# Decode step, one core: w_down's last rows on all partitions, wo's last row product sent straight to the output rows, and no closing barrier

## The chip, the cores and the metric

One core of one Trainium2 chip. The metric is the device time of one execution in microseconds (us); a kernel's figure is the median of its runs. With one core there is no second die to compare. Every change that this document talks about is below 0.4% of the time, so two instruments are used side by side: medians of runs taken in the same rounds, and distances between events in the trace of one execution.

Some words that are used throughout. A semaphore is a counter on which an engine waits. A transfer has landed when the last of its parts (sixteen for each weight) has been counted on its semaphore. A matmul keeps one operand (the weights) in the tensor engine and streams the columns of the other, the moving operand, past it; its results go to PSUM. The granted clock is the share of the tensor engine's full clock that the profile records.

## The reference

```python
x  = A_x                                   # 1 x 1 x 640
xn = layernorm(x)
q  = (xn @ wq)                             # 32 heads of 128
p  = softmax(q @ k_cache^T * 128**-0.5)    # 32 heads, 32768 keys each
o  = p @ v_cache
h  = silu(xn @ w_gate) * (xn @ w_up)       # 1728 hidden units
out = x + o @ wo + h @ w_down              # 1 x 1 x 640, bf16
```

The caches of keys and values are 8 MB per head each, 537 MB together, and are read once. All the rest is small: wq 5.2 MB, w_gate and w_up 2.2 MB each, w_down 2.2 MB, wo 5.2 MB.

## The kernel before

The kernel streams the caches through a ring of three 64 KB slots per partition. After the last head comes a tail: the feed-forward weights (gate, up, down), then wo in six pieces, are read into the same ring, and the products end in one 128x5 accumulator `acc` (5 columns of 128 outputs). These are the parts that the change touches.

```python
    WTAIL = [8, 8, 8, 5, 2, 1]            # wo: rows per partition in each piece, 32 in all
    ...
    # DMA queue, tail. 1728 = 13 * 128 + 64, so FM = 13, FL = 64, FB = 14
    e.dma_start(wg, ...).then_inc(s_ffn[0], 16)
    e.dma_start(wu, ...).then_inc(s_ffn[1], 16)
    e.dma_start(flat[:, d0:d0 + FM * D], B_w_down[0:FM * 128, :].rearrange(
        "(p j) n -> p (j n)", j=FM)).then_inc(s_ffn[2], 16)
    e.dma_start(wd[0:FL, FM, :], B_w_down[FM * 128:F, :]).then_inc(s_ffn[2], 16)   # 64 partitions
    ...                                                         # then wo, piece by piece
    e.wait_ge(s_fin, 2)
    e.dma_start(out[...], orow[:, :]).then_inc(s_out, 16)

    # tensor engine, tail
    hidden_part(0); ...; hidden_part(1); down(); project().then_inc(s_att, 1)
    def project():
        for i, n in enumerate(WTAIL):
            t.wait_ge(s_wo[i], 16)
            for _ in range(n):
                for c in range(NCD):       # NCD = 5; the moving operand has one column
                    mm = t.matmul(acc[:, c:c + 1], lhsT=wo_v[:, j, c, :], rhs=ot[:, j:j + 1], ...)
                j += 1
    t.wait_ge(s_fin, 1)
    t.matmul(orow_ps, lhsT=outb[:, :], rhs=ident[:, :], start=True, stop=True).then_inc(s_or, 1)  # turn

    # vector engine, tail
    v.wait_ge(s_att, 1)
    v.tensor_tensor(out=outb[:, :], in0=xr[:, :], in1=acc, op=ALU.add).then_inc(s_fin, 1)
    v.wait_ge(s_or, 1)
    v.tensor_copy(out=orow[:, :], in_=orow_ps).then_inc(s_fin, 1)

    # GpSimd, end
    g.wait_ge(s_out, 16)                   # the output has landed; then a barrier of all engines
```

## Time and profile before

| | before |
|---|---|
| median of 3 runs | 1288.11 us (1288.03 to 1288.64) |
| span in the profile | 1286.3 us |
| read from HBM | 553.99 MB, 431 GB/s over the span |
| busy share: tensor, vector, scalar engine | 81%, 52%, 4% |

The first lines are from the page of the kernel before. Each row of the first two cuts the span into 40 slices: the granted clock of the tensor engine in tenths, then GB/s. The third is the chain of waits, by engine.

```profile
PEclk9799888898888999888898888898888998888895
...
GB/s 424 424 450 427 429 438 431 430 430 444 428 432 442 428 432 434 436 428 432 442 430 432 436 432 430 430 444 428 432 442 428 432 432 438 428 432 442 430 417 355
...
DMA 53%; PE 30%; DVE 11%; issue 6%; DVEq 0%; SPq 0%
```

The DMA rate is level from the first slice to the 38th (424 to 450 GB/s). Only the last two slices sag (417, 355), and in the last one the granted clock falls to 0.5. The page's row of DMA shares, in tenths, reads 9 in every slice but the last, which is 8. So the place to look for a gain without reading less is the end, the last 64 us.

The table of stretches of the kernel before, for the tail (start:end and length in us, then busy time and instruction count of each engine, granted clock, DMA share, GB/s):

```profile
core 0: us, PE busy (x) PEld busy (x) DVE busy (x) ACT busy (x) POOL busy (x), PEclk, DMA share, GB/s
1260.00:1265.00 5.00, 4.79 (x128) 4.70 (x128) 0.51 (x2) 0.00 (x0) 0.00 (x0) 0.50 1.01 426
1265.00:1270.00 5.00, 3.62 (x59) 3.60 (x60) 0.00 (x0) 0.20 (x1) 0.00 (x0) 0.50 1.00 380
1270.00:1275.00 5.00, 3.52 (x73) 3.45 (x72) 0.93 (x8) 0.23 (x2) 0.00 (x0) 0.50 0.98 398
1275.00:1280.00 5.00, 3.63 (x130) 3.52 (x127) 0.00 (x0) 0.00 (x0) 0.00 (x0) 0.50 1.00 415
```

The DMA engines are busy throughout (share 0.98 to 1.01), but between 1265 and 1275 they move less: 380 and 398 GB/s. That is where w_down arrives. A share near 1 says that engines have packets under way, not that they move bytes at their best rate.

The end of the chain of waits of the kernel before, in order of time (start, length in us, what):

```profile
1253.07 29.08 DMA ring<-in_A_wo_dram
1282.15 0.05 issue
1282.19 1.49 PE ps L414 x40
1283.68 0.03 issue
1283.71 0.05 DVEq L602
1283.76 0.04 issue
1283.81 0.17 DVE outb L603
1283.98 0.04 issue
1284.02 0.28 PE ps L439
1284.30 0.02 issue
1284.33 0.28 DVE orow L605
```

L414 are the 40 matmuls of wo's last three pieces, L603 the sum with x, L439 the turn from 128x5 to 5x128, L605 the copy out of PSUM. The view merges the last three pieces into one DMA wait; by the semaphore records of the trace they landed at 1282.15, 1282.93 and 1283.33. The same records put the output's landing at 1285.82, GpSimd's sight of it at 1285.85 and the end of the closing barrier at 1286.26. The last semaphore record of the execution, which belongs to the runtime and not to the kernel, is at 1288.18; the measured time of this execution was 1288.06.

### The profile page before, as it was taken

How to read it: one execution, taken by the hardware profiler on the slowest of the kernel's cores; microseconds unless marked ns; L12 is line 12 of the kernel's file. 1: busy time of each engine (PE TensorE's matmuls, PEld its weight loads, DVE VectorE, ACT ScalarE, POOL GpSimd, SP SyncE). 2: the span in 40 equal slices, each digit the busy share in tenths (PEclk: the TensorE clock that was granted, in tenths of full speed). 3: DMA queues.
4: the chain of work that ended last, by engine and by line, in shares of the span. 5: the costliest groups of instructions: out<-in, count | busy, mean ns of one | idle time of the engine just before them, and what ended most of it. 6: DMA issues, size and time to landing. Idle time of an engine off the chain costs nothing.

```text
span 1286.3 us, 9864 instructions
## 1 busy us (share of the span) xinstructions
PE 1041.6 (81%) x5153; PEld 261.4 (20%) x3234; DVE 670.4 (52%) x409; ACT 52.2 (4%) x140; POOL 2.5 (0%) x17
## 2 busy tenths in 40 slices
PE   4599777789777788777798777788777798778797
PEld 1011112221112221112221112221112221112227
DVE  0855665445665445664446664446664446654440
ACT  2000000000000000000000000000000000000000
POOL 0000000000000000000000000000000000000000
PEclk9799888898888999888898888898888998888895
DMA  9999999999999999999999999999999999999998
GB/s 424 424 450 427 429 438 431 430 430 444 428 432 442 428 432 434 436 428 432 442 430 432 436 432 430 430 444 428 432 442 428 432 432 438 428 432 442 430 417 355
DMA packets 11192, 554.17 MB, mean 431 GB/s; under 512 B 1259, under 2 KB 1452, under 8 KB 1708
## 3 DMA queue, kind: packets, MB, share of 16 engines
q1 hardware_dynamic: 11178, 554.00, 99.7%
q8 instruction: 9, 0.15, 0.0%
q14 instruction: 3, 0.02, 0.0%
q10 hardware_dynamic: 2, 0.00, 0.0%
HBM read 553.99 MB, written 0.00 MB: 431 GB/s over the span
## 4 chain that ended last, share of the span: by engine, by line
DMA 53%; PE 30%; DVE 11%; issue 6%; DVEq 0%; SPq 0%
DMA ring<-in_A_k_cache_dram 51%; PE ps L327 17%; PE ps L295 11%; DVE ring L543 10%; DMA ring<-in_A_wo_dram 2%; PE ps L314 1%; PE ps L369 0%; PE ps L363 0%; PE ps L357 0%; PE ps L414 0%; SPq L239 0%; DVEq L543 0%; DVE sc L549 0%; DVE pmax L555 0%; DVEq L188 0%
## 5 line engine op out<-in xcount | busy, mean ns | idle before, releaser
L543 DVE TENSOR_TENSOR ring<-ring,qb 128x8192 bf16<-128x8192 bf16 x128 | 557.8, 4420 | 316.4 <-DMA ring<-in_A_k_cache_dram 316.4
L295 PE MATMUL ps<-ring,ident 128*128 128x512 bf16 x1920 | 496.4, 417 | 0.0
L327 PE MATMUL ps<-ring,P 128*4 128x512 bf16 x1984 | 443.3, 379 | 0.0
L314 PE MATMUL ps<-ring,ident 128*128 128x512 bf16 x128 | 55.9, 437 | 220.7 <-DVE ring L543 220.2
L327 PEld LDWEIGHTS ps<-ring,P 128*4 128x4 bf16 x1984 | 163.4, 85 | 237.8
L314 PEld LDWEIGHTS ps<-ring,ident 128*128 128x128 bf16 x128 | 12.6, 98 | 618.0 <-DVE ring L543 345.0
L549 DVE TENSOR_REDUCE sc<-ps 128x64 f32<-128x512 f32 x128 | 82.3, 684 | 62.6 <-PE ps L295 62.6
L561 DVE TENSOR_SCALAR negb<-ps 128x1 f32<-128x1 f32 x32 | 5.1, 158 | 108.4 <-PE ps L369 108.4
L466 ACT ACTIVATE P<-sc,negb 128x256 bf16<-128x256 f32 x32 | 16.2, 507 | 956.7 <-DVE negb L561 956.7
L558 DVE TENSOR_REDUCE m<-ps 1x1 f32<-1x128 f32 x32 | 8.9, 278 | 85.2 <-PE ps L363 85.2
L349 PEld LDWEIGHTS ps<-identf,o 4*128 4x128 f32 x248 | 30.6, 190 | 13.1 <-issue 13.1
L349 PE MATMUL ps<-identf,o 4*128 4x1 f32 x248 | 33.2, 251 | 0.0
L357 PEld LDWEIGHTS ps<-rsum,ones 128*128 128x128 f32 x64 | 12.1, 190 | 99.0 <-issue 98.2
L457 ACT ACTIVATE o<-ps,rzb 4x512 f32<-4x512 f32 x31 | 21.0, 678 | 6.2 <-PE ps L327 6.2
L287 PE MATMUL ps<-ring 128*128 128x512 bf16 x39 | 11.3, 458 | 10.9 <-DMA ring<-in_A_wq_dram 10.9
L462 ACT ACTIVATE ocol<-ps 128x1 f32 (+1 forms) x31 | 5.4, 173 | 222.2 <-PE ps L349 222.2
L555 DVE TENSOR_REDUCE pmax<-sc 128x1 f32<-128x256 f32 x32 | 13.4, 420 | 0.0
L363 PE MATMUL ps<-identf,pmax 128*1 128x128 f32 x64 | 12.2, 273 | 1.2 <-DVE pmax L555 1.2
L369 PE MATMUL ps<-m,ones 1*128 1x1 f32 x64 | 12.1, 256 | 0.4 <-DVE m L558 0.4
L369 PEld LDWEIGHTS ps<-m,ones 1*128 1x128 f32 x64 | 9.4, 182 | 14.2 <-issue 13.5
L393 PE MATMUL ps<-xn,ring 128*128 128x1 bf16 (+1 forms) x140 | 8.9, 198 | 1.6 <-issue 1.6
L531 DVE RECIPROCAL rzb<-ps 128x1 f32<-128x1 f32 x32 | 5.1, 159 | 8.1 <-PE ps L357 8.1
(62 smaller groups left out, 80.8 us busy)
## 6 DMA issues: line engine op xcount, KB each, us to landing
ring<-in_A_wq_dram SPq DMA_DIRECT2D x1, 5120.0 KB, 15.3
ring<-in_A_v_cache_dram SPq DMA_DIRECT2D x1, 4096.0 KB, 31.8
ring<-in_A_wo_dram SPq DMA_DIRECT2D x3, 1280.0 KB, 25.0
ring<-in_B_w_gate_dram SPq DMA_DIRECT2D x1, 2160.0 KB, 22.9
ring<-in_B_w_up_dram SPq DMA_DIRECT2D x1, 2160.0 KB, 27.7
ring<-in_B_w_down_dram SPq DMA_DIRECT2D x1, 2080.0 KB, 31.7
ring<-in_A_v_cache_dram SPq DMA_DIRECT2D x1, 2048.0 KB, 36.4
ring<-in_A_v_cache_dram SPq DMA_DIRECT2D x2, 1024.0 KB, 39.4
```

Source lines behind the costliest of these rows:

```text
L295: return t.add_instruction(mybir.InstMatmult(start_tensor_calc=False, stop_tensor_calc=stop, tile_size=(128, 128), tile_position=(0, 0), l ...
L314: t.matmul(ob, lhsT=ident[:, :], rhs=src, start=True, stop=False)
L327: mm = t.matmul(O, lhsT=P[:, h % PR, j:j + W], rhs=ring[:, s, j * DH:(j + W) * DH], start=(j == 0), stop=(j + W == NJ))
L349: mm = t.matmul(fold_ps, lhsT=o4[:, m * DH:(m + 1) * DH], rhs=identf[0:W, m:m + 1], start=(m == 0), stop=(m == W - 1))
L357: t.matmul(misc[:, 129:130], lhsT=ones[:, :], rhs=rsum[:, h % SR:h % SR + 1], start=True, stop=True).then_inc(s_z, 1)
L363: t.matmul(misc[0:1, 0:128], lhsT=pmax[:, h % SR:h % SR + 1], rhs=identf[:, :], start=True, stop=True).then_inc(s_t, 1)
L369: t.matmul(misc[:, 128:129], lhsT=ones[0:1, :], rhs=m1[0:1, h % SR:h % SR + 1], start=True, stop=True).then_inc(s_b, 1)
L457: a.activation(out=o4[:, :], in_=O, func=ACTF.Copy, scale=rzb[0:W, h % SR:h % SR + 1]).then_inc(s_o4, 1)
L466: a.activation(out=P[:, h % PR, :], in_=sc[:, :], func=ACTF.Exp, bias=negb[:, h % SR:h % SR + 1], scale=c_scale, accum_out=rsum[:, h % SR: ...
L543: v.tensor_tensor(out=kh, in0=kh, in1=q[:, None, :].to_broadcast([128, HF, DH]), op=ALU.mult).then_inc(s_mul, 1)
L549: v.tensor_reduce(out=sc[:, i * HF:(i + 1) * HF], in_=bank[i].rearrange("p (j e) -> p j e", e=G), axis=AX.X, op=ALU.add).then_inc(s_red, 1)
L555: v.tensor_reduce(out=pmax[:, h % SR:h % SR + 1], in_=sc[:, :], axis=AX.X, op=ALU.max).then_inc(s_max, 1)
```

## The change

Three things, in one diff:

1. **w_down's last 64 rows.** Each row of 640 is split into two halves, so that 64 rows become 128 half rows on all 128 partitions. The hidden units that multiply them must then stand twice, once per half; the vector engine makes doubled copies of the last 64 columns of w_gate and w_up so that the matmul delivers them that way. A mask of zeros and ones (`par`) then keeps each half row to its own half of the outputs.
2. **wo's last row.** The product of the last piece (one row per partition) no longer goes into the columns of `acc`. Five matmuls with 128 moving columns write it straight into the 5x128 output rows, and the turned sum of all the rest is added there. The intent is that the sum on the vector engine no longer stands behind the last landing.
3. **No closing barrier.** The instructions of the program's last block are emptied.

```diff
-        e.dma_start(wd[0:FL, FM, :], B_w_down[FM * 128:F, :]).then_inc(s_ffn[2], 16)
+        e.dma_start(wdr, B_w_down[FM * 128:F, :].rearrange(
+            "f (t n) -> (f t) n", t=2)).then_inc(s_ffn[2], 16)
 ...
+    def twice(i):                                   # vector engine
+        v.wait_ge(s_ffn[i], 16)
+        v.tensor_copy(out=wt[i].rearrange("p c (f t) -> p c f t", t=2),
+                      in_=(wg_v, wu_v)[i][:, :, FM * 128:F][:, :, :, None].to_broadcast(
+                          [128, NCD, FL, 2])).then_inc(s_twice, 1)
 ...  (the vector stages of silu, one instruction each instead of two, but for the last; down() in halves)
-    for i, n in enumerate(WTAIL):
+    for i, n in enumerate(WTAIL[:-1]):
 ...
+    def rows():
+        t.wait_ge(s_dg, 1)
+        t.wait_ge(s_wo[-1], 16)
+        for c in range(NCD):                        # dg: the last column of ot, one 128x5 block per c
+            t.matmul(orow_ps, lhsT=dg[:, c * NCD:(c + 1) * NCD], rhs=wo_v[:, OC - 1, c, :],
+                     start=(c == 0), stop=False, skip_group_check=True)
+        t.wait_ge(s_fin, 1)
+        return t.matmul(orow_ps, lhsT=accs[:, :], rhs=identf[:, :], start=False, stop=True,
+                        skip_group_check=True)      # accs is fp32
 ...
-    t.wait_ge(s_fin, 1)
-    t.matmul(orow_ps, lhsT=outb[:, :], rhs=ident[:, :], start=True, stop=True).then_inc(s_or, 1)
+    rows().then_inc(s_or, 1)
 ...
+    nc.main_func.blocks[-1].instructions = []
```

## The prediction

> **What bounds the kernel.** DMA. The page gives a DMA share of 9 in every slice and 431 GB/s over a span of 1286.3 us; 553.99 MB are read, and the change reads the same bytes. So only the last 25 us can change. There the chain of waits ends: wo's DMA (to 1282.15), 1.49 us of matmuls for its last 8 rows, the sum with x on the vector engine, one matmul that turns it, a copy, the output DMA. From the trace: wo's last three pieces land at 1282.15, 1282.93 and 1283.33; the 5 matmuls of the last piece end at 1283.68, the sum at 1283.98, the turn at 1284.30, the copy at 1284.62; the output DMA lands at 1285.82; the closing barrier ends at 1286.26. The other 1.9 us are the runtime's.
>
> **1. w_down's last 64 rows (the largest term).** The table of stretches shows 426 GB/s in 1260-1265, 380 in 1265-1270, 398 in 1270-1275, 424 in 1275-1278. The dip is where the 64-partition transfer of w_down runs: in the packet records the 10240-byte packets then take 490-517 ns instead of 389, those of 16640 bytes up to 807 instead of 622. The Trainium skill, "SBUF — State Buffer", section on the DMA port swizzle, says partitions 0 to 63 reach only 8 of 16 ports. The dip agrees. At the rates before and after it (gate to up 5.15 us for 2160 KB, wo pieces 3.09 us for 1280 KB) wo's first piece should have landed on its slowest engine at about 1273.4, but landed at 1274.01. Estimate: 0.57 us earlier for every later landing, net of twice as many packets of half the size (0.03). It lies wholly on the critical path, since wo's landings are waited for.
>
> **2. Direct last row.** Removed: 5 matmuls of about 27 ns and the vector engine's sum behind the last landing. Added behind it: 5 matmuls with 128 moving columns, and an fp32 turn of two passes in place of one bf16 pass. The granted clock is 0.50 there. The bf16 turn (128 columns) took 0.27 us, one with 1 column 0.165, so 0.105 us per 128 columns. An fp32 pass started 0.110 us after the other at clock 1.00; estimate 0.21 each at 0.50. After the last landing: 0.04 + 5x0.107 + 2x0.21 + 0.18 = 1.18 us, against 0.97 before (1283.33 to 1284.30). So this part loses 0.2 us.
>
> **3. No closing barrier.** GpSimd sees the output at 1285.85; the barrier ends at 1286.26. The runtime keeps its own (the Trainium skill, "Runtime: NRT & Kernel Launch", preamble/postamble breakdown). Gain 0.3 us, as the branch stays; between 0.15 and 0.6.
>
> **Off the path.** FFN matmuls and their vector stages: one instruction per stage saves about 0.2 us, but the tensor engine waits 1.6 us for wo afterwards. The duplicating copies (0.8 us each, as the 640-element copy at the start) fit idle time.
>
> **Sum:** -0.57 + 0.2 - 0.3 = about -0.7 us: 1287.4 us, range 1286.8 to 1288.1. Faster by over 2%: 0.005; same: 0.99; slower: 0.005.
>
> **Would show it right:** about 420 GB/s through 1265-1275; wo's last landing near 1282.8; the turn's end about 1.2 us after it; no barrier after GpSimd's last wait. **Wrong:** dip still there (not ports); landing-to-turn under 0.97 us (the row really is a gain); an instruction-fetch stall ("issue" idle, 0.5 to 1.6 us in this tail) moving behind the last landing; end-to-end gain from the barrier nil.

## The result, and the profile after

| | before | after |
|---|---|---|
| median of 4 runs each, same rounds | 1288.07 us (1287.97 to 1288.64) | 1287.62 us (1287.51 to 1287.67) |
| span in the profile | 1286.3 us | 1285.7 us |

The ratio is 0.9995, with a 95% interval of 0.9978 to 1.0013: by that the two are the same. All four runs after lie below all four before; a later repeat in other rounds gave 1287.68 against 1288.06. The gain is about 0.4 us, a thirtieth of one per cent.

The page of the kernel after, the same three lines:

```profile
PEclk9799888898888898888998888898888998888995
...
GB/s 424 425 451 427 427 436 437 430 428 444 428 430 438 434 432 426 444 428 430 438 434 432 426 444 428 430 442 430 432 428 442 428 430 444 430 430 428 444 412 362
...
DMA 53%; PE 29%; DVE 11%; issue 6%; DVEq 0%; SPq 0%
```

Nothing moved in the body of the kernel, as intended. The stretches of the tail:

```profile
core 0: us, PE busy (x) PEld busy (x) DVE busy (x) ACT busy (x) POOL busy (x), PEclk, DMA share, GB/s
1260.00:1265.00 5.00, 4.56 (x123) 4.47 (x120) 1.34 (x3) 0.00 (x0) 0.00 (x0) 0.50 1.02 433
1265.00:1270.00 5.00, 4.11 (x72) 4.12 (x73) 1.01 (x2) 0.20 (x1) 0.00 (x0) 0.50 0.97 405
1270.00:1275.00 5.00, 3.54 (x100) 3.48 (x99) 1.04 (x6) 0.18 (x1) 0.00 (x0) 0.50 1.01 422
1275.00:1280.00 5.00, 3.02 (x101) 2.83 (x98) 0.00 (x0) 0.00 (x0) 0.00 (x0) 0.50 1.00 414
```

From 380 and 398 the rate rose to 405 and 422. The extra 25 and 24 GB/s over 5 us each are 0.25 MB, which at 430 GB/s is 0.57 us.

The end of the chain of waits:

```profile
1253.28 28.38 DMA ring<-in_A_wo_dram
1281.65 0.05 issue
1281.70 1.23 PE ps L431 x35
1282.92 0.04 issue
1282.96 0.69 PE ps L440 x5
1283.65 0.44 PE ps L443 x2
1284.09 0.02 issue
1284.12 0.28 DVE orow L635
```

The wo DMA now ends 0.50 us earlier (1281.65 for 1282.15). The sum on the vector engine has left the chain, as was intended. But L440 (the five wide matmuls, 0.69 us) and L443 (the fp32 turn, two instructions, 0.44 us more) have come in. The timeline of the kernel after shows the same three side by side (start, length, engine, line, operation, count, and in brackets the idle time before it with what ended it):

```profile
1282.96 0.69 PE L440 MATMUL ps<-ring,dg 128*5 128x128 bf16 x5
1283.03 0.16 DVE L633 TENSOR_TENSOR accs<-xr,ps 128x5 f32<-128x5 f32 x1 [9.84 <-PE ps L431]
...
1283.45 0.63 PE L443 MATMUL ps<-identf,accs 128*5 128x128 f32 x2
```

The sum is done at 1283.19, while the tensor engine still streams the wide matmuls until 1283.65. Hiding the sum worked, but what took its place is longer: from the last landing to the end of the turn it is 1.27 us, for 0.97 before (next table).

To compare many kernels, the tail is cut at five events read from the semaphore records of each trace: w_up's last landing, wo's last landing, the end of the turn, GpSimd's sight of the output, and the last record of the execution (us):

| kernel | up to wo's last landing | last landing to turn | turn to GpSimd's sight | sight to last record |
|---|---|---|---|---|
| before | 18.19 | 0.97 | 1.54 | 2.33 |
| after | 17.58 | 1.27 | 1.54 | 2.16 |
| difference | -0.61 | +0.30 | 0 | -0.17 |

The three parts of the change fall into three different columns. They sum to -0.48; w_up itself landed 0.10 later in the profiled execution after, so the last record came 0.39 us earlier (1287.79 for 1288.18).

### The profile page after: what moved, and what is told of

It reads as the page before. It is cut to its first block, busy times and chain, and to the rows that moved or that the text cites. A ratio compares the mean times of both kernels' runs of the same rounds, so it can differ in the third digit from the quotient of the medians.

```text
span 1285.7 us, 9856 instructions
## 1 busy us (share of the span) xinstructions
PE 1045.5 (81%) x5155; PEld 261.5 (20%) x3236; DVE 672.3 (52%) x410; ACT 52.1 (4%) x139; POOL 2.6 (0%) x18
## 4 chain that ended last, share of the span: by engine, by line
DMA 53%; PE 29%; DVE 11%; issue 6%; DVEq 0%; SPq 0%
DMA ring<-in_A_k_cache_dram 51%; PE ps L340 17%; DVE ring L566 11%; PE ps L308 10%; DMA ring<-in_A_wo_dram 2%; PE ps L327 1%; PE ps L382 0%; PE ps L376 0%; PE ps L370 0%; PE ps L431 0%; SPq L251 0%; DVEq L566 0%; DVE sc L572 0%; PE ps L440 0%; PE ps L443 0%
## 5 line engine op out<-in xcount | busy, mean ns | idle before, releaser
L406 PE MATMUL ps<-xn,ring 128*128 128x1 bf16 x140 | 8.4, 196 | 1.3 <-issue 1.3
```

## The experiments

All twelve kernels gave correct results. Theory A is the prediction's: w_down gains through the SBUF ports, the row form loses at the half clock, the barrier gains a little. Rivals: B, the barrier alone gives the measured gain; C, the row form is a gain; D, the barrier gives nothing; E and F, the DMA dip is not about partitions but about bytes or packet sizes; G, the order of the waits and not the clock sets the row form's cost.

### Each part alone, and the change without its row part

Edits: the first has only hunk 1 of the diff above, the second only hunk 2, the third only hunk 3. The fourth has hunks 1 and 3:

```diff
 (against after)
-    for i, n in enumerate(WTAIL[:-1]):
+    for i, n in enumerate(WTAIL):
 ...
-    rows().then_inc(s_or, 1)
+    t.wait_ge(s_fin, 1)
+    t.matmul(orow_ps, lhsT=outb[:, :], rhs=ident[:, :], start=True, stop=True).then_inc(s_or, 1)
```

What was expected of w_down alone:

> Only w_down's last rows on all partitions (with the copies and hidden units on 128 rows that it needs); the last row of wo stays in columns and the closing barrier stays. Theory A (ports): 0.57 us faster than before, about 1287.5; the dip to 380 and 398 GB/s in 1265-1275 is gone, wo's last landing lies near 1282.8, and landing to turn stays 0.97 us. Rival B (the barrier alone gives the 0.45 us that was measured): within 0.1 us of before.

Of the row alone:

> Only wo's last row straight to output rows. Theory A: the five wide matmuls and the fp32 turn run at half clock, so last landing to end of turn grows from 0.97 to about 1.26 us and the kernel is 0.3 us slower than before, about 1288.4. Rival C (the row form is a gain, as its authors meant, since the sum leaves the tail): last landing to turn below 0.97 us and the time below before's.

Of the barrier alone:

> Only the closing barrier removed. Theory A: from GpSimd's sight of the output to the end 2.33 us in before, 2.16 us in after, so 0.17 us faster than before, about 1287.9, the rest of the trace unchanged. Rival B: 0.45 us faster. Rival D (the runtime's own barrier takes as long): no change, within 0.05 us.

Of the change without the row part:

> After without the row part: w_down on all partitions and no closing barrier, the last row in columns as before. Theory A: 0.29 us faster than after, about 1287.3, so faster than both kernels; landing to turn back to 0.97 us. Rival C: slower than after.

Measured, five runs each beside nine of before on the same chip (before: 1288.14 us, 1287.83 to 1288.23):

| kernel | median (range), us | to before | up to last landing | landing to turn | sight to last record |
|---|---|---|---|---|---|
| w_down alone | 1287.46 (1287.28 to 1287.57) | -0.68 | 17.61 | 0.95 | 2.33 |
| row alone | 1288.31 (1288.19 to 1288.45) | +0.17 | 18.32 | 1.27 | 2.33 |
| no barrier alone | 1287.83 (1287.65 to 1287.96) | -0.31 | 18.21 | 0.97 | 2.16 |
| w_down and no barrier | 1287.24 (1287.16 to 1287.57) | -0.90 | 17.60 | 0.94 | 2.25 |

Each part moves its own column of the trace, and the other columns stay within 0.13 us of before. The 2.25 in the last row is such a deviation: over all fourteen traces this column reads 2.33 with the closing barrier (once 2.42) and 2.16 without it (twice 2.24 to 2.25). w_down is the gain (rival B falls: the barrier alone gives less than half of what w_down gives, and w_down gains with the barrier in place). The row form costs 0.30 us in the trace; in the time it costs 0.17 us here, which the runs of this round alone would hardly separate from noise, so it was tested once more below. Rival C falls by the trace. The barrier is worth 0.17 us in the trace and 0.2 to 0.3 us in the medians; D falls.

The medians do not add up as the columns do. Alone, the parts make -0.68, +0.17 and -0.31, in sum -0.82, while the whole change measured -0.45. In the fourteen traces w_up's landing, before which no part of the change acts on the DMA queue, lies anywhere from 1264.90 to 1265.35; that spread enters every time, but no column. So the sizes of the parts are taken from the columns, and a difference of medians below some 0.3 us is not read as a size.

### Why w_down gained: partitions, bytes or packet size

First, the disputed transfer is issued five times instead of once, in each of its two forms (the copies land in unused columns):

```diff
 (against before)
         e.dma_start(wd[0:FL, FM, :], B_w_down[FM * 128:F, :]).then_inc(s_ffn[2], 16)
+        for i in range(4):
+            u = d0 + (FB + i) * D
+            e.dma_start(flat[0:FL, u:u + D], B_w_down[FM * 128:F, :]).then_inc(s_ffn[2], 16)
 (against after)
+        for i in range(4):
+            u = u0 + 2 * NCD * 128 + i * (D // 2)
+            e.dma_start(flat[:, u:u + D // 2], B_w_down[FM * 128:F, :].rearrange(
+                "f (t n) -> (f t) n", t=2)).then_inc(s_ffn[2], 16)
```

> Before, with the transfer of w_down's last 64 rows to partitions 0 to 63 issued five times in place of once (four more into unused columns of the same partitions, 0.33 MB more). Theory A (ports): each such transfer costs 0.6 to 0.8 us of landing time, of which 0.19 is its bytes, so 2.4 to 3.2 us slower than before, about 1291. Rival E (the dip has nothing to do with this transfer, only the bytes count): 0.8 to 0.9 us slower, 1289.

> After, with its transfer of w_down's last rows to all 128 partitions issued five times in place of once (the same 0.33 MB more, in packets of 640 bytes). Theory A: each costs its bytes and its packets' overhead alone, 8 packets of 32 ns on each engine, 0.26 us, so 1.0 us slower than after, about 1288.7. A dip like before's, or 2.4 us, would say that small transfers as such are slow and the partitions are not the cause.

Second, the 64 partitions of before are kept but the packets made as short as those of after:

```diff
 (against before)
+        wdg = flat[0:FL, w0:w0 + 2 * 384].rearrange("p (t n) -> p t n", t=2)[:, :, 0:D // 2]
 ...
-        e.dma_start(wd[0:FL, FM, :], B_w_down[FM * 128:F, :]).then_inc(s_ffn[2], 16)
+        e.dma_start(wdg, B_w_down[FM * 128:F, :].rearrange(
+            "f (t n) -> f t n", t=2)).then_inc(s_ffn[2], 16)
 ...  (the matmuls read the two halves)
```

> Before, with the 64 rows still on partitions 0 to 63 but each in two packets of 640 bytes (the halves lie 128 bytes apart in the row). It has after's packet size and before's partitions. Theory A (ports): the dip stays, 10240-byte packets near 500 ns in 1268-1270, up's landing to wo's last landing stays at 18.2 us, the time within 0.15 us of before. Rival F (the packet size or the packet count cured it): dip gone, 17.6 us, 0.6 us faster.

Measured beside nine runs of before (1288.03 us, 1287.96 to 1288.57):

| kernel | median (range), us | up to wo's first piece landed | up to wo's last |
|---|---|---|---|
| before (trace above) | | 8.87 | 18.19 |
| 64 partitions, five times | 1292.32 (1292.07 to 1293.32) | 12.05 | 22.23 |
| after (trace above) | | 8.30 | 17.58 |
| 128 partitions, five times | 1288.51 (1288.33 to 1288.53) | 9.18 | 18.58 |
| 64 partitions, packets of 640 bytes | 1288.13 (1288.06 to 1288.23) | 8.90 | 18.23 |

Up to wo's first piece, four more transfers to 64 partitions cost 3.18 us, 0.80 each; four more to 128 partitions cost 0.88 us, 0.22 each. The bytes alone, 82 KB at 430 GB/s, are 0.19. The one transfer of the change should then gain 0.80 - 0.22 = 0.58, and it gained 8.87 - 8.30 = 0.57. The five-fold kernel was 4.29 us slower than before, where 0.8 to 0.9 us were expected of rival E, which falls, and 2.4 to 3.2 us of theory A, which was too low as well (see below). Rival F falls too: short packets on 64 partitions leave time and landings where they were.

The stretches, of 64 partitions five times, then of 128 five times, then of 64 with short packets:

```profile
1265.00:1270.00 5.00, 3.57 (x58) 3.54 (x59) 0.00 (x0) 0.20 (x1) 0.00 (x0) 0.50 1.00 330
1270.00:1275.00 5.00, 3.40 (x67) 3.30 (x67) 0.93 (x8) 0.23 (x2) 0.00 (x0) 0.50 1.03 245
1275.00:1280.00 5.00, 2.95 (x97) 2.71 (x93) 0.00 (x0) 0.00 (x0) 0.00 (x0) 0.50 1.01 423
```

```profile
1265.00:1270.00 5.00, 4.23 (x74) 4.24 (x75) 0.94 (x2) 0.20 (x1) 0.00 (x0) 0.50 0.99 395
1270.00:1275.00 5.00, 3.54 (x100) 3.47 (x99) 1.03 (x6) 0.18 (x1) 0.00 (x0) 0.50 1.03 427
```

```profile
1265.00:1270.00 5.00, 4.19 (x68) 4.16 (x69) 0.00 (x0) 0.20 (x1) 0.00 (x0) 0.50 1.02 379
1270.00:1275.00 5.00, 3.51 (x83) 3.44 (x82) 0.93 (x8) 0.23 (x2) 0.00 (x0) 0.50 0.96 394
```

With five transfers the dip deepens to 245 GB/s at an unchanged DMA share of 1.03, and ends with the transfers (423 in the next stretch). Short packets on 64 partitions give the dip of before almost to the digit (379, 394 for 380, 398). The packet records show that the large packets of the neighbouring transfers are slow while the small ones run. Mean time of one packet in ns, worked out from those records (4 to 33 packets for each figure of a kernel), for packets that start from 1268 to 1269 us (w_down's main part, 16640 bytes) and from 1269 to 1270 us (wo's first piece, 10240 bytes):

| kernel | 16640 bytes | 10240 bytes |
|---|---|---|
| undisturbed | 622 | 389 |
| before (64 partitions) | 807 | 517 |
| 64 partitions, short packets | 786 | 537 |
| 64 partitions, five times | 1198 | 841 |
| after (128 partitions) | 621 | 388 |
| 128 partitions, five times | 620 | 385 |

The five-fold kernel lost 4.3 us, more than the 3.2 us of its landings up to wo's first piece. The rest is at the very end: its last wo piece landed 1.26 us after the one before it (0.40 in before). Thirteen of its sixteen parts had landed by 1286.32 and fifteen by 1286.64, the last only at 1287.49. An instruction fetch of 16384 bytes ran on the DMA engines from 1285.21 to 1286.31. That it sat in front of that one part is a guess; the records do not name the engine.

### Why the row form lost: columns at half the clock

The turn is made in bf16 instead of fp32, one pass for two:

```diff
 (against after)
-        accs = sbt("accs", [128, NCD], F32)
+        accs = sbt("accs", [128, NCD], BF16)
 ...
-        return t.matmul(orow_ps, lhsT=accs[:, :], rhs=identf[:, :], start=False, stop=True, ...)
+        return t.matmul(orow_ps, lhsT=accs[:, :], rhs=ident[:, :], start=False, stop=True, ...)
```

> After, with the turned sum in bf16: one pass of 128 columns in place of two fp32 passes. Theory A (the row form pays for columns at half clock): a pass of 0.107 in place of two of 0.213 us, landing to turn falls from 1.26 to about 0.95 us, 0.3 us faster than after, about 1287.3, level with the kernel that has no row part. If the vector engine's sum or something else were what ends last there, nothing changes.

Measured: 1287.39 us (1287.23 to 1287.57), in the rounds of the three kernels above, 0.64 below before. Landing to turn fell from 1.27 to 0.95 us as expected. So the tensor engine's columns were what ended last. The row form then costs as much as the column form (0.95 against 0.94 to 0.97), which is no gain either. So at an unchanged clock of 0.50 what the fp32 turn takes beyond a bf16 turn (0.32 us) accounts for the whole loss; the half clock sets what each column costs, but is not by itself what made this form lose.

The other half of the theory is the clock. In two kernels, the tensor engine is given work while it waits, so that the full clock may be granted at the end:

```diff
 (against after, and against the bf16 turn)
+    def busy(n):
+        for _ in range(n):
+            t.matmul(bank[1], lhsT=ident[:, :], rhs=qb[:, 0:512], start=True, stop=True)
 ...
     def down():
         t.wait_ge(s_ffn[2], 32)
+        busy(3)
 ...
         for i, n in enumerate(WTAIL[:-1]):
+            busy({2: 7}.get(i, 0))
             t.wait_ge(s_wo[i], 16)
```

> After, with matmuls of 512 columns into an unused bank where the tensor engine waits anyway: 3 before the hidden units are ready, 7 before wo's third piece. They are meant to have the clock granted at 1.00 at the end. Theory A (the row form loses because its columns run at half clock): where the profile shows 1.00 behind the last landing, the wide matmuls start 0.056 apart instead of 0.107 and the turn's passes 0.110 instead of 0.213, landing to turn falls from 1.26 to about 0.75 us, 0.5 us faster than after, 1287.1. If the clock stays at 0.50: nothing changes, since all ten fit into waits (1.4 and 1.85 us, then 0.7). Rival G (the order of the waits, not the clock, sets landing to turn): 1.26 us even at clock 1.00.

> The same ten matmuls in the kernel with the bf16 turn. Theory A: at clock 1.00 landing to turn is about 0.56 us (0.04, six matmuls at 0.056, 0.18) against 0.95 without them, 0.4 us faster than that kernel, about 1287.0, and faster than the kernel without the row part, since only then is the row form the cheaper one. At clock 0.50: level with the bf16 turn alone.

Measured beside before at 1288.19 us (1287.93 to 1288.39): 1289.47 us with the fp32 turn and 1288.76 us with the bf16 turn, both slower than before. The expectation that the ten matmuls fit into waits was wrong. The tensor engine's timeline of the first shows why:

```profile
1275.35 2.31 PE L437 MATMUL ps<-ot,ring 128*128 128x1 bf16 x79
1279.39 0.18 PE L437 MATMUL ps<-ot,ring 128*128 128x1 bf16 x1 [1.74 <-issue]
1279.43 3.15 PE L412 MATMUL ps<-qb,ident 128*128 128x512 bf16 x7
```

The wait before wo's third piece was not free. 1.74 us of it is "issue", an engine that waits for nothing the profile shows; it ends after an instruction fetch of 16384 bytes (1277.03 to 1278.09 in the DMA records). The fillers stood behind that stall and began at 1279.43, and by the time they were through, at 1282.4, the third and fourth piece had long landed (1279.48, 1281.46).

As a measurement of the clock the pair still worked, because only the second was granted it in its profiled execution. Why the first was not, with the same ten matmuls, no run shows. Its stretches (columns as above):

```profile
1282.00:1284.00 2.00, 2.00 (x61) 1.68 (x59) 0.00 (x0) 0.00 (x0) 0.00 (x0) 0.72 0.05 12
1284.00:1286.00 2.00, 1.11 (x29) 0.81 (x25) 0.44 (x2) 0.00 (x0) 0.00 (x0) 1.00 0.00 0
```

The end of the timeline, first of the bf16 turn alone (clock 0.50), then of the bf16 turn with fillers (clock 1.00):

```profile
1282.84 0.69 PE L440 MATMUL ps<-ring,dg 128*5 128x128 bf16 x5
...
1283.33 0.31 PE L443 MATMUL ps<-ident,accs 128*5 128x128 bf16 x1
```

```profile
1284.49 0.44 PE L446 MATMUL ps<-ring,dg 128*5 128x128 bf16 x5
1284.67 0.16 DVE L639 TENSOR_TENSOR accs<-xr,ps 128x5 bf16<-128x5 f32 x1 [11.65 <-PE ps L437]
...
1284.89 0.22 PE L449 MATMUL ps<-ident,accs 128*5 128x128 bf16 x1
```

At full clock the five wide matmuls take 0.44 us instead of 0.69 (they start 0.055 us apart instead of 0.107) and the turn 0.22 instead of 0.31. From the first wide matmul to the end of the turn it is 0.63 us against 0.81. The gain is 0.18 and not the 0.3 that six matmuls at 0.056 us instead of 0.107 make, because now the sum on the vector engine ends last: the turn starts at 1284.89, just after the sum's end at 1284.84. Where the clock stayed at 0.50, in the fp32 kernel with fillers, that stretch took 1.13 us, as in after. So the clock carries 0.18 us of that stretch, and rival G falls as it was stated (no change at clock 1.00); with those 0.18 us gone, the wait for the sum is what ends last, as it would have it. This rests on one execution at full clock. Whether a row form with both the full clock and no delayed data would beat the column form end to end is open.

### After and the version without the row part, in the same rounds

> The changed kernel itself, unchanged, on one chip and in the same rounds as the version without the row part, which so far was only compared with it across rounds. Theory A: 0.45 us faster than before.

> W_down on all partitions and no closing barrier, wo's last row in columns. Theory A: 0.3 us faster than the changed kernel of the same rounds (landing to turn 0.95 against 1.26 us), 0.8 us faster than before. If it is not faster than the changed kernel by at least 0.15 us here, the row part's cost is not shown in the time, only in the trace.

Measured, five runs each: after 1287.68 us (1287.44 to 1287.77), without the row part 1287.28 us (1287.19 to 1287.48), before 1288.06 us (nine runs, 1287.81 to 1288.29). Landing to turn was 1.27 and 0.94 us. The version without the row part is 0.40 us faster than the change and 0.78 us faster than before. All its runs lie below all of before's; its slowest (1287.48) is above the fastest of after (1287.44), but the 0.33 us between 1.27 and 0.94 stands in the traces too.

## Why the prediction was right, and where its sizes were off

The prediction was 1287.4 us, 1286.8 to 1288.1; measured 1287.62. That the total lies inside says little, since the range reaches up to before's own 1288.07 and two of the misses below (the row form and the barrier) add up rather than cancel; the three columns are the test. There the chain held: each of its three terms has the right sign, and stands in the column where it was expected.

- **w_down: predicted -0.57, measured -0.61** from w_up's landing to wo's last (-0.57 up to wo's first piece). wo's last landing was put near 1282.8 and came at 1282.83. The Trainium skill, "SBUF — State Buffer", section on the DMA port swizzle, says that partitions 0 to 63 reach only 8 of 16 ports. The runs agree that the partitions matter and not bytes or packet size (the kernel with short packets on 64 partitions did not gain, five transfers cost 0.80 us each). They do not show the port map itself: no run put the 64 rows on other halves of the partitions. The stretch 1265-1270 reached 405 GB/s, not the 420 that was named.
- **Row form: predicted +0.2, measured +0.30.** The columns were sized right: wide matmuls 0.107 us apart, fp32 passes 0.213. What was mis-sized is the term of 0.04 us between landing and the first of them. It took 0.14 us (1282.83 to 1282.96), since two waits stand in front of it and the one for the landing became an instruction of its own (1282.86 to 1282.91 in the trace). The matmuls of before started 0.05 us after it (1283.33 to 1283.38). The other terms came within 0.05 us of their estimates and cancel. Testing for the diagonal before wo's last pieces might save these 0.09 us; that is a guess, and was not run.
- **Barrier: predicted -0.3, measured -0.17** in the trace of the kernel after. The step that failed reads "as the branch stays": what the barrier took on its own (1285.85 to 1286.26, 0.41 us) was taken for what would be saved, less the branch. The runtime's own end, which the Trainium skill's "Runtime: NRT & Kernel Launch" lists under the preamble/postamble breakdown, still follows and gave part of it back: from the end of the barrier to the last record it took 1.92 us before, and in the kernel after, from the jump with which GpSimd leaves its part of the program, 2.06 us, so that the end came 0.17 us sooner. Why it takes longer is not shown. The barrier is not nil, which the prediction had named as a way to be wrong.
- **Off the path:** the hidden units were ready 1.1 us earlier than before (the last stage started at 1272.83, not 1273.94), but not for the reason given. From the last matmul of the hidden units to the first with w_down it took 1.47 us, for 1.48 before, so the predicted 0.2 us of one instruction per stage did not come; the hidden units' own matmuls ended 1.03 us earlier (1271.80 for 1272.83), which was not traced further. It was worth nothing either way: the tensor engine waited 1.85 us for wo's third piece afterwards, for 1.61 before. The doubling copies took 0.82 us each, as estimated, in idle time.
- **Sum:** predicted -0.7, measured -0.45 (-0.38 in the repeat). The difference is the 0.1 of the row form and the 0.13 of the barrier.

## What to carry to other kernels

A transfer to partitions 0 to 63 cost more than its bytes here (0.80 us for 0.19): it slowed the transfers around it, at a DMA share that still read 1.0. Look for a sag in GB/s, and try such a remainder folded over all 128 partitions. Before work is moved out of a chain, cost what takes its place at the clock that is granted there: 0.34 us around a sum and 0.31 us of narrow matmuls left the chain, and 0.49 us of wide matmuls, a turn longer by 0.36 us and a start later by 0.09 us came in. When a change has several parts, run each alone; here one part gave more than the whole, and the change without its weakest part is faster than the change.

## What the Trainium skill lacked or had wrong

- "SBUF — State Buffer", section on the DMA port swizzle: it gives the rate of a transfer to 64 partitions by itself, not what it does to others in a full queue. Here 82 KB cost 0.80 us against 0.22 on 128 partitions, and other transfers' packets of 10240 bytes took 517 ns instead of 389 while it lasted.
- "TensorE: Matmul & The Clock Gate", section on the clock gate: it does not say there that the clock can fall to half during a stream of matmuls with one column and a weight load each. From 1252.9 to 1256.1 in the trace of before the tensor engine ran 128 of them without a pause, and at 1256.3 the granted clock fell to 0.50 and stayed there. In the other traces it fell between 1254.0 and 1256.7. That such a stream counts as idle is a guess. Its gap of 107 ns cold for 128 columns agrees with the trace (0.107 us); at full clock it was 0.055.
- "Runtime: NRT & Kernel Launch", section on instruction fetch: it calls the crossing of a 16 KB block mostly hidden. With the DMA engines full of data, the tensor engine of before stood idle for "issue" at three places of its straight-line tail, a multiple of about 256 instructions apart, for 0.34 to 1.59 us each. Each of these waits ended 1.4 to 1.6 us after the end of a fetch of 16384 bytes in the DMA records. In the first kernel with fillers there was one of 1.74 us. That the fetch is what was waited for is argued from this order alone.
- The same page, preamble/postamble breakdown: it does not say what a closing barrier of the program's own adds to the runtime's. Here it was 0.17 us in the trace (2.33 for 2.16).
